# The rows of the first expert slot: gathers, stores and loads put two steps earlier, four weight pieces put later

## The chip, the cores and the metric

The kernel runs on one core of a Trainium2 chip. The metric is device time in microseconds (us), the median of several runs. The engines are named as in the profile: PE (matrix multiply), PEld (its weight loads), DVE (vector), ACT (scalar), POOL (GpSimd) and SP (the queue that issues most DMAs). Each works through its own instructions in order, and they wait for each other through semaphores.

## What is computed

Banded attention over 8 batches, 8 heads, 576 positions and 64 dimensions, then a mixture of 8 experts of which each token takes one:

```python
scores = where(mask[h], q @ k.T / 8, -1e9)      # 4 heads: window of 32; 4 heads: every 4th of 128 back
x = softmax(scores) @ v                          # -> [4608 tokens, 512]
logits = x @ w_gate + modality_bias[modality_id]
e = argmax(logits); g = max softmax(logits)
out[i] = g[i] * (relu(x[i] @ w1[e[i]]) @ w2[e[i]])   # w1: [8, 512, 1024], w2: [8, 1024, 512]
```

## The kernel before

**Attention.** The work is cut into 72 units, nine per batch; a unit is up to 128 query rows of a few heads. A step handles two units; `state['t']` is the number of the first, so it counts 0, 2, 4, ... 70, and "step 64" below is the step in which it is 64. In step t the scores of units t, t+1 are made and masked (`sm`, L438, the first DVE work of a step), those of the step before go through exp (ACT, L448), and those of two steps before are multiplied with v and normalized into `x_sb` (L399). `x_sb` has three buffers; a buffer is stored to `x_dram` in DRAM by a POOL DMA at the step's end, and the DVE may write it again only when that store has landed. The DMAs of q and k (`st`) and of v (`vw`) for the next batch are issued on SP in the same steps. After each batch its tokens are routed: the gate's logits, ranks per expert, and six POOL scatters (L632) of token numbers into `table`, one row range per expert.

**Experts.** The second phase works through slots of 256 tokens of one expert; 18 slots and a half one. Four slots are fixed early, from the first three batches. A slot's rows take this path, all in `gather`: token numbers `idt` come from `table`; four POOL DMAs gather rows of `x_dram` into `xr` (128 rows by 256 floats each); one DMA stores `xr` to `x_slot` in DRAM (512 KB); four DMAs load it back as `xg` in another layout (128 KB each). Then `prepare_x` makes the operands: for each half of the slot a DVE transpose `xt` from `xg` (L963), an ACT cast `xh` (L969) and a DVE difference `xl` (L972). For slots 0 and 1 all DMAs of `gather` are on POOL. PE multiplies `xh`, `xl` with halves of the weights (L1097, L1015); weights come by SP into `w1q` (two tiles, four pieces each for the first slot) and `w2q` (four tiles), `fetch_weights`. From step 70 on expert work is mixed with the last attention steps.

**What sets the order.** PE, DVE, ACT and SP run in the order in which the program is written; POOL too, through a chain of ordering edges. Each step calls the batch tasks three times (`advance`). One of them, `background(2)`, runs three generators side by side: `first_rows(0, ...)` and `first_rows(1, ...)`, which take the next part of `gather` when `state['t']` has reached the next number of their lists, and `first_slot`, which issues one weight piece of slot 0 at each number of its list. With `t0 = (b + 2) * 9 + 6` = 42 the list of `first_rows(0)` is 54, 55, 58, 59, 60, 62, 64: four gathers, an empty part, the store to `x_slot`, the loads of `xg`. Odd numbers come at the next even step. The twelve pieces of `first_slot` are `w2q` 0, `w1q` 0 in four parts, `w2q` 1, `w2q` 2, `w1q` 1 in four parts, `w2q` 3. DMAs of a queue take eight landing semaphores in turn, so an issue waits until the eighth DMA before it on that queue has landed.

Of the kernel before, what the change touches and what calls it, by code (L numbers as in the profile page):

```python
# [58 lines left out]
def kernel(  # L59
# [64 lines left out]
    def load_qk(b, kd, queue=nc.sync):  # L124
        kn = load_one(b, kd, k)
        return load_one(b, kd, q, queue), kn
# [24 lines left out]
    state = {('qk', 0, 0): load_qk(0, 0, nc.scalar)}  # L151
# [581 lines left out]
    def rest_info():  # L733

        eh, bh, cs = state['rest']
        yield
        state['info_h'] = yield from slot_list(eh, bh, 1, "info_h", False)
        yield
        nc.vector.memset(state['info', len(EARLY)][:, 2, NSTAT:NSTAT + 1], 1)
        state['left'] = cpool.tile([1, 1], I32, name="left")  # L740
        nc.vector.tensor_scalar(out=state['left'], in0=cs[:, 0, NE - 1:NE], scalar1=float(-NSTAT), scalar2=0.0, op0=ALU.add, op1=ALU.max)
# [51 lines left out]
    def gather(n, ids):  # L793


        idt, nu = ids
        xr = gat.tile([P, 2, DM], F32, name="xr", bufs=1)
        nrows = round_rows(n)
        queue = pool if n < 2 else nc.sync
        for u in range(nu):  # L800
            for kd in range(2):
                pool.indirect_dma_start(out=xr[:, u, 256 * kd:256 * kd + 256], out_offset=None, in_=x_dram[kd][0:nrows, :],
                                        in_offset=bass.IndirectOffsetOnAxis(ap=idt[:, u, 2 * kd:2 * kd + 1], axis=0),
                                        bounds_check=nrows - 1, oob_is_err=False)
                yield
        yield
        queue.dma_start(out=x_slot[0:P * nu, :].rearrange("(u p) c -> p u c", p=P), in_=xr[:, 0:nu])
        yield
        while 0 < n < NS and n - 1 not in taken:
            yield  # L810
        xg = gat.tile([P, 2 * KC, P], F32, name="xg", bufs=1)
        for r in range(KC):
            queue.dma_start(out=xg[BLK * r:BLK * (r + 1), 0:nu * KC],
                              in_=x_slot[0:P * nu, P * r:P * (r + 1)].rearrange("(g i) c -> i g c", i=BLK))
        state['xg', n] = xg
# [31 lines left out]
    ids_of, si_of, fetching, loads_of = {}, {}, [], {}  # L847
# [8 lines left out]
    def fetch_slot(n):  # L856

        queue = pool if n == 1 or n in round_from else nc.sync
        if n == NS - 1:
            if 'info_h' not in state:  # L860
                return False
            si_of[n] = slot_regs(state['info_h'], 0)
        else:
            r = max(r for r, n0 in enumerate(round_from) if n >= n0)
            if ('info', r) not in state:
                return False
            si_of[n] = slot_regs(state['info', r], n - round_from[r])
        ids_of[n] = fetch_ids(si_of[n], state['scatters'] if n == NEARLY else (), 1 if n == NS - 1 else 2, queue, n < NEARLY)
        return True

    def load_more(n, pieces):

        if n not in loads_of and n in si_of:
            loads_of[n] = [fetch_weights(si_of[n], n == 0), 0]
        if n in loads_of:
            for _ in range(min(pieces, 6 - loads_of[n][1])):
                next(loads_of[n][0], None)
                loads_of[n][1] += 1

    def first_rows(n, at):  # L880

        rows = gather(n, ids_of[n])
        for t in at:
            while state['t'] < t:
                yield
            next(rows, None)
            yield
        fetching.extend([(n, rows)] * n)
        todo['rows'] = max(todo['rows'], n + 1)

    def first_slot():

        prep = prepare_x(0, ids_of[0])
        for n, at in enumerate((46, 50, 52, 54, 56, 60, 62, 64, 65, 66, 67, 68)):
            while state['t'] < at:
                if state['t'] > 63:
                    next(prep, None)
                yield
            load_more(0, 1)
            loads_of[0][1] = max(n - 5, 1)  # L900
            yield
        yield from prep

    def background(b):


        if b < B - 1:
            yield
            yield
        steps = gating(b, state['lT', b])  # L910
        if b in round_of:
            for _ in steps:
                yield
                if ('counts', b) in state:
                    break
            yield from together(steps, slot_info(state['counts', b], round_of[b]))
            if round_of[b] > 0:
                return
            yield
            for n in range(2):  # L920
                fetch_slot(n)
                yield

            t0 = (b + 2) * 9 + 6
            yield from together(first_rows(0, (t0 + 12, t0 + 13, t0 + 16, t0 + 17, t0 + 18, t0 + 20, t0 + 22)), first_rows(1, (t0 + 21, t0 + 22, t0 + 24, t0 + 25)), first_slot())
            while state['t'] < NU - 4:
                yield
            state['go'] = True
            return
        yield from steps  # L930
        if b == B - 1:
            yield
            yield from slot_info(state['counts', b], len(EARLY))
            yield from rest_info()
            state['routed'] = True
# [6 lines left out]
    def together(*pieces):  # L942

        pieces = list(pieces)
        while pieces:
            for p in list(pieces):
                if next(p, pieces) is pieces:
                    pieces.remove(p)
            yield


    def prepare_x(n, ids):


        nu = ids[1]
        while ('xg', n) not in state:
            yield
        xg = state['xg', n]
        xh = xpre.tile([P, KC, SLOT], F32R, name="xh")
        xl = xpre.tile([P, KC, SLOT], F32R, name="xl")  # L960
        for u in range(nu):
            xt = xpre.tile([P, KC, P], F32, name="xt", bufs=1)
            nc.vector.transpose(out=xt.rearrange("p m (g i) -> p g m i", i=BLK),  # L963
                                in_=xg[:, KC * u:KC * (u + 1)].rearrange("p g (m c) -> p g m c", c=BLK))
            if u == nu - 1:
                taken.add(n)
            yield
            ts = slice(P * u, P * (u + 1))
            nc.scalar.copy(out=xh[:, :, ts], in_=xt)  # L969
            if n == 0:  # L970
                yield
            nc.vector.tensor_tensor(out=xl[:, :, ts], in0=xt, in1=xh[:, :, ts].bitcast(F32), op=ALU.subtract)  # L972
            if u < nu - 1:
                yield
        state['x', n] = xh, xl
# [249 lines left out]
    for t in range(NPAIR + 4):  # L1225
# [49 lines left out]
        n = NCHUNK[here[0][1]] if here and t > 1 else (0, 0)  # L1275
# [4 lines left out]
        for one in late:  # L1280
            one.gather_logits()
            if one.last:
                tasks.append((one.b, background(one.b)))
# [75 lines left out]
```

## Time and profile before

| | |
|---|---|
| median of 3 runs | 673.14 us (671.59 to 675.19) |
| the profiled execution | 676.78 us, of which its span (first to last instruction) 675.2 us |
| mean granted TensorE clock | 0.984 |
| PE, PEld busy | 635.6 us (94%), 553.1 us (82%) |
| DVE, ACT, POOL busy | 478.8, 433.5, 250.5 us |
| moved by DMAs | 99.12 MB, mean 147 GB/s |

Attention takes the first third of the span, the experts the rest. The busy shares are means over both. The profile cuts the span into 40 slices of 16.9 us; the step times and waits of the place that the change touches are read from the trace, from 140 to 262 us. Granted clock 1.00 is the higher of the two levels of TensorE's clock (2.4 GHz), 0.50 the lower (1.2 GHz).

### The profile page before, as it was taken

Reading aid. Unit: us, or ns where it says so; the run is one execution under the profiler, and the core shown is the slowest. Engines: PE = TensorE matmul, PEld = TensorE weight load, DVE = VectorE, ACT = ScalarE, POOL = GpSimd, SP = SyncE. Lnnn points to the kernel's source line nnn. Section 1 sums busy time; section 2 is a strip of 40 time slices with the busy share of each in tenths; the row PEclk is TensorE's granted clock in tenths of the full one; section 3 lists DMA queues with packets and bytes.
Section 4 is the critical chain, followed back from the end, with each engine's and each line's share of the span. In section 5 each row is a group of like instructions: output and inputs, shape, how many; then the busy total and the mean of one; then the engine's idle time right before and its main releaser. Section 6 shows DMA issues by size and latency. Waiting matters only on the chain. (4 is left out here: it accounts for less than half of the span.)

```text
span 675.2 us, 17669 instructions
## 1 busy us (share of the span) xinstructions
PE 635.6 (94%) x6398; PEld 553.1 (82%) x6398; DVE 478.8 (71%) x1068; ACT 433.5 (64%) x1002; POOL 250.5 (37%) x348
## 2 busy tenths in 40 slices
PE   7989999999994899999999999999999999999994
PEld 3778788888873787889999999999999999999973
DVE  3778868888773777956776677667766776677653
ACT  1778888888873665456566656665666566556653
POOL 8032344555664386735231321332313241321110
PEclk8999999999996999999999999999999999999998
DMA  9987776999995243965332237823222335931560
GB/s 181 211 227 184 201 155 167 204 183 234 222 274 142 72 91 123 191 163 164 110 110 80 79 111 228 209 79 110 95 95 79 109 110 147 246 108 56 136 175 13
DMA packets 121998, 99.12 MB, mean 147 GB/s; under 512 B 67424, under 2 KB 99682, under 8 KB 121908
## 3 DMA queue, kind: packets, MB, share of 16 engines
q1 hardware_dynamic: 106724, 66.56, 41.9%
q0 software_dynamic: 12144, 30.75, 15.0%
q8 instruction: 51, 0.84, 0.6%
q10 hardware_dynamic: 3040, 0.65, 0.6%
q14 instruction: 39, 0.32, 0.2%
HBM read 127.52 MB, written 29.39 MB: 232 GB/s over the span
## 5 line engine op out<-in xcount | busy, mean ns | idle before, releaser
L982 DVE TENSOR_TENSOR w2l<-w2q,w2h 128x512 fp32r<-128x512 f32 x152 | 104.4, 689 | 40.3 <-ACT w2h L981 32.3
L1015 PE MATMUL py<-w2h,hh 128*128 128x512 f32 x288 | 115.1, 400 | 0.5 <-ACT ys L1018 0.5
L313 POOL DMA_INDIRECT xr<-x_dram,idt x74 | 81.1, 1096 | 89.8 <-DMA x_slot<-xr 67.5
L1015 PE MATMUL py<-w2h,hl 128*128 128x512 f32 x288 | 113.5, 394 | 0.0
L1015 PE MATMUL py<-w2l,hh 128*128 128x512 f32 x288 | 112.3, 390 | 0.0
L313 POOL DMA_INDIRECT out_dram<-ys,idt x37 | 40.7, 1101 | 188.3 <-ACT ys L1018 123.6
L982 DVE TENSOR_TENSOR w1l<-w1q,w1h 128x512 fp32r<-128x512 f32 x152 | 103.7, 684 | 8.9 <-ACT w1h L981 8.8
L981 ACT CAST w1h<-w1q 128x512 fp32r<-128x512 f32 x152 | 94.1, 622 | 3.5 <-DMA w1q<-in_moe_w_dram 3.1
L981 ACT CAST w2h<-w2q 128x512 fp32r<-128x512 f32 x152 | 92.7, 613 | 0.0
L1097 PE MATMUL pt<-xh,w1h 128*128 128x256 f32 x304 | 86.2, 284 | 0.0
L1097 PE MATMUL pt<-xh,w1l 128*128 128x256 f32 x304 | 85.8, 282 | 0.2 <-DVE w1l L982 0.2
L1097 PE MATMUL pt<-xl,w1h 128*128 128x256 f32 x304 | 85.5, 281 | 0.0
L448 ACT ACTIVATE sm<-sm,nmx 128x96 f32<-128x96 f32 x288 | 80.5, 370 | 4.2 <-DVE nmx L444 4.2
L1103 ACT ACTIVATE hh<-pt 128x256 fp32r<-128x256 f32 x76 | 29.1, 384 | 80.7 <-PE pt L1097 80.7
L1097 PE MATMUL ph<-xh,w1l 128*128 128x256 f32 x272 | 76.7, 282 | 1.6 <-DVE w1l L982 1.6
L1097 PE MATMUL ph<-xh,w1h 128*128 128x256 f32 x272 | 76.7, 282 | 0.1
L1097 PE MATMUL ph<-xl,w1h 128*128 128x256 f32 x272 | 76.5, 281 | 0.0
L1103 ACT ACTIVATE hh<-ph 128x256 fp32r<-128x256 f32 x68 | 26.0, 383 | 71.7 <-PE ph L1097 71.7
L632 POOL DMA_INDIRECT table<-pay,dst x48 | 49.6, 1033 | 45.1 <-DVE pay L625 22.4
L1015 PEld LDWEIGHTS py<-w2l,hh 128*128 128x128 f32 x288 | 54.1, 188 | 13.4
L1015 PEld LDWEIGHTS py<-w2h,hh 128*128 128x128 f32 x288 | 54.7, 190 | 8.0 <-ACT ys L1018 0.9
L1097 PEld LDWEIGHTS pt<-xh,w1h 128*128 128x128 f32 x304 | 57.4, 189 | 3.4
(218 smaller groups left out, 1336.8 us busy)
## 6 DMA issues: line engine op xcount, KB each, us to landing
w2q<-in_moe_w_dram SPq DMA_DIRECT2D x76, 512.0 KB
w1q<-in_moe_w_dram SPq DMA_DIRECT2D x152, 256.0 KB
x_dram<-x_sb POOLq DMA_DIRECT2D x32, 256.0 KB
x_slot<-xr SPq DMA_DIRECT2D x16, 512.0 KB
xg<-x_slot SPq DMA_DIRECT2D x64, 128.0 KB
st<-in_k_dram SPq DMA_DIRECT2D x32, 144.0 KB
vw<-in_v_dram SPq DMA_DIRECT2D x16, 288.0 KB
st<-in_k_dram SPq DMA_DIRECT2D x8, 576.0 KB
```

The costliest lines, as they stand in the source:

```text
L313: ins = tc.keep_in_program_order(getattr(nc.gpsimd, name)(*args, **kw))
L448: nc.scalar.activation(out=self.sm[:, j], in_=self.sm[:, j], func=AF.Exp, bias=self.nmx[:, j])
L632: ins = nc.gpsimd.indirect_dma_start(out=table, out_offset=bass.IndirectOffsetOnAxis(ap=dst[:, c:c + 1], axis=0), in_=pay[:, b * NGB + c, ...
L981: nc.scalar.copy(out=hi, in_=raw)
L982: nc.vector.tensor_tensor(out=lo, in0=raw, in1=hi.bitcast(F32), op=ALU.subtract)
L1015: nc.tensor.matmul(out=py[u], lhsT=ht[:, us], rhs=wt, start=(f + n == 0), stop=(f + n == FC + 1))
L1097: nc.tensor.matmul(out=ph, lhsT=wt[:, c, :], rhs=xt[:, c, 0:cols], start=(c + i == 0), stop=(c + i == KC + 1))
L1103: nc.scalar.activation(out=hh, in_=ph, func=AF.Relu)
```

## The change

```diff
     def first_slot():
 
-        prep = prepare_x(0, ids_of[0])
-        for n, at in enumerate((46, 50, 52, 54, 56, 60, 62, 64, 65, 66, 67, 68)):
+        for n, at in enumerate((46, 50, 52, 54, 56, 62, 64, 64, 66, 66, 68, 68)):
             while state['t'] < at:
-                if state['t'] > 63:
-                    next(prep, None)
                 yield
             load_more(0, 1)
             loads_of[0][1] = max(n - 5, 1)
             yield
-        yield from prep
+
+    def first_x():
+
+        while state['t'] < 64:
+            yield
+        yield from prepare_x(0, ids_of[0])
...
-            yield from together(first_rows(0, (t0 + 12, t0 + 13, t0 + 16, t0 + 17, t0 + 18, t0 + 20, t0 + 22)), first_rows(1, (t0 + 21, t0 + 22, t0 + 24, t0 + 25)), first_slot())
+            yield from together(first_rows(0, (t0 + 8, t0 + 9, t0 + 10, t0 + 12, t0 + 13, t0 + 14, t0 + 18)), first_rows(1, (t0 + 21, t0 + 22, t0 + 24, t0 + 25)), first_slot(), first_x())
```

The list of `first_rows(0)` becomes 50, 51, 52, 54, 55, 56, 60: each part of `gather` for slot 0 comes two steps (four units) earlier or three (the store). `prepare_x` runs as a generator of its own, from step 64 on. The pieces `w2q` 1 and `w2q` 2 go from steps 60 and 62 to 62 and 64. Nothing is added or left out: 303 rows on POOL, 754 on SP, as before.

On POOL, from the last gather of slot 0 to its loads `xg` (steps 60 to 64), before:

```order
L313 DMA xr<-x_dram_88,idt 128x256
L632 DMA table<-pay,dst 41472x3
L313 DMA x_dram_87<-x_sb 128x2x256
L632 DMA table<-pay,dst 41472x3
L313 DMA x_slot<-xr 128x2x512
L632 DMA table<-pay,dst 41472x3
L313 TENSOR_TENSOR t_3918<-t_3918,ewt 96x48
L313 TENSOR_TENSOR ex<-l,mx 96x48
L313 DMA x_dram_87<-x_sb 64x256
L313 DMA x_dram_88<-x_sb 32x2x128 x2
L632 DMA table<-pay,dst 41472x3
L313 DMA xg<-x_slot 32x8x128 x4
```

and now, from step 56 (`sume` is a small sum of the routing) to step 60:

```order
L313 TENSOR_SCALAR sume<-sume 96x6
L313 DMA x_slot<-xr 128x2x512
L313 TENSOR_TENSOR r_3577<-oh 96x24
L313 TENSOR_TENSOR run<-run,r_3577 96x8 x3
L313 TENSOR_TENSOR t_3574<-t_3574,oh 96x48
L313 DMA x_dram_88<-x_sb 128x2x256
L632 DMA table<-pay,dst 41472x3
L313 DMA x_dram_87<-x_sb 128x2x256
L632 DMA table<-pay,dst 41472x3
L313 DMA xg<-x_slot 32x8x128 x4
L632 DMA table<-pay,dst 41472x3
L313 DMA x_dram_87<-x_sb 128x2x256
```

The four gathers stand ahead of this piece; the last of them stands where the first stood, and `xg` stands where the last gather stood, ahead of the store of `x_sb` that ends the piece.

On DVE, from the `nmx` of step 64 to the first `xl`, before:

```order
L444 TENSOR_REDUCE nmx<-sm 128x8
L469 TENSOR_SCALAR den<-po 128x8
L470 RECIPROCAL den<-den 128x8
L399 TENSOR_TENSOR x_sb<-po,den 128x2x2x64 x2
L514 COPY lT<-po 64x4x32
L514 COPY lT<-po 64x4x16
L518 TENSOR_TENSOR lT<-po,lT 64x2x32
L149 COPY vw_109<-vw_109 32x520 x2
L963 STREAM_TRANSPOSE xt<-xg 128x4x4x32
L584 TENSOR_REDUCE m_4053<-t_3918 96x6
L586 TENSOR_TENSOR oh<-ewt,m_4053 96x48
L972 TENSOR_TENSOR xl<-xt,xh 128x4x128
```

and now, from the `sm` of step 64:

```order
L438 TENSOR_TENSOR sm<-pss,masks 128x768
L965 STREAM_TRANSPOSE xt<-xg 128x4x4x32
L444 TENSOR_REDUCE nmx<-sm 128x8
L469 TENSOR_SCALAR den<-po 128x8
L470 RECIPROCAL den<-den 128x8
L399 TENSOR_TENSOR x_sb<-po,den 128x2x2x64 x2
L514 COPY lT<-po 64x4x32
L514 COPY lT<-po 64x4x16
L518 TENSOR_TENSOR lT<-po,lT 64x2x32
L149 COPY vw_109<-vw_109 32x520 x2
L974 TENSOR_TENSOR xl<-xt,xh 128x4x128
L584 TENSOR_REDUCE m_4054<-t_3922 96x6
```

The transpose has moved from the end of step 64 to just behind the step's `sm`; the second one moves likewise, to just ahead of the `sm` of step 66.

On SP, the loads of steps 58 to 62, before:

```order
L121 DMA st<-in_k_dram 96x4x384
L121 DMA st<-in_q_dram 96x4x384
L833 ISA
L833 DMA w2q_246<-in_moe_w_dram 128x2x512
L141 DMA vw_107<-in_v_dram 64x4x128 x2
L141 DMA vw_107<-in_v_dram 16x4x128
L141 DMA vw_107<-in_v_dram 48x4x128
L141 DMA vw_107<-in_v_dram 64x4x128
L141 DMA vw_107<-in_v_dram 32x4x128
L833 ISA
L833 DMA w2q_247<-in_moe_w_dram 128x2x512
```

and now:

```order
L121 DMA st<-in_k_dram 96x4x384
L121 DMA st<-in_q_dram 96x4x384
L141 DMA vw_107<-in_v_dram 64x4x128 x2
L141 DMA vw_107<-in_v_dram 16x4x128
L141 DMA vw_107<-in_v_dram 48x4x128
L141 DMA vw_107<-in_v_dram 64x4x128
L141 DMA vw_107<-in_v_dram 32x4x128
L833 ISA
L833 DMA w2q_246<-in_moe_w_dram 128x2x512
L833 ISA
L833 DMA w2q_247<-in_moe_w_dram 128x2x512
```

One weight tile of 512 KB has gone behind the last v loads of attention; the rest of SP's order is the same. PE's order is the same from end to end.

## Rows read from the trace of the kernel before

**Rows 1.** The page, the span in 40 slices: PE's busy tenths and granted clock.

```profile
PE   7989999999994899999999999999999999999994
PEclk8999999999996999999999999999999999999998
```

**Rows 2.** Waits, 150 to 262 us: who waited for whom, total, times, longest.

```profile
DVE xt L963 <- DMA xg<-x_slot: 9.7, 1, 9.7
...
DVE x_sb L399 <- DMA x_dram<-x_sb: 3.1, 2, 1.9
...
POOL table L632 <- DMA table<-pay,dst: 1.2, 1, 1.2
```

**Rows 3.** Timeline of DVE: start, us, instruction, [idle before it <-what ended that].

```profile
195.02 0.42 DVE L399 TENSOR_TENSOR x_sb<-po,den 128x256 f32<-128x256 f32 x1 [1.23 <-DMA x_dram<-x_sb]
...
197.98 0.96 DVE L438 TENSOR_TENSOR sm<-pss,masks 128x768 f32<-128x768 f32 x1 [0.75 <-ACT ux L482]
...
200.27 0.75 DVE L399 TENSOR_TENSOR x_sb<-po,den 128x256 f32<-128x256 f32 x2
...
212.11 0.71 DVE L963 STREAM_TRANSPOSE xt<-xg 128x512 f32<-128x512 f32 x1 [9.72 <-DMA xg<-x_slot]
```

**Rows 4.** Timeline of POOL, same columns; a DMA's us are its issue.

```profile
172.00 1.12 POOL L313 DMA_INDIRECT xr<-x_dram,idt  x1 [0.30 <-issue]
...
177.90 0.24 POOL L313 TENSOR_SCALAR sume<-sume 96x6 f32<-96x6 f32 x1
...
185.64 0.78 POOL L313 DMA_DIRECT2D x_dram<-x_sb  x1
186.72 0.96 POOL L632 DMA_INDIRECT table<-pay,dst  x1 [0.30 <-issue]
187.99 1.05 POOL L313 DMA_INDIRECT xr<-x_dram,idt  x1 [0.30 <-issue]
...
190.28 0.78 POOL L313 DMA_DIRECT2D x_dram<-x_sb  x1
...
196.16 0.74 POOL L313 DMA_DIRECT2D x_slot<-xr  x1 [3.84 <-DMA xr<-x_dram,idt]
...
204.05 2.35 POOL L313 DMA_DIRECT2D xg<-x_slot  x4 [2.41 <-DMA x_slot<-xr]
```

**Rows 5.** Steps 46, 48, 50; 62, 64, 66, 68: length, busy times, PEclk, DMA share, GB/s.

```profile
145.60:150.84 5.24, 5.24 (x104) 4.44 (x102) 4.89 (x19) 5.24 (x16) 3.44 (x7) 1.00 0.87 222
150.84:155.74 4.90, 4.90 (x105) 4.35 (x103) 4.43 (x12) 4.47 (x13) 1.97 (x8) 1.00 0.96 210
155.74:160.45 4.71, 4.71 (x102) 4.16 (x100) 4.51 (x14) 4.62 (x14) 0.73 (x1) 1.00 1.18 256
...
189.55:197.98 8.43, 6.98 (x115) 5.66 (x116) 4.77 (x13) 4.75 (x14) 3.97 (x5) 1.00 1.11 259
197.98:214.11 16.13, 6.89 (x144) 5.80 (x140) 5.88 (x15) 6.41 (x19) 9.65 (x15) 0.78 0.90 243
214.11:220.12 6.01, 5.98 (x63) 4.92 (x65) 4.96 (x15) 4.52 (x13) 2.25 (x8) 0.50 0.00 0
220.12:225.40 5.28, 5.28 (x111) 4.50 (x110) 5.08 (x15) 4.28 (x13) 1.14 (x2) 0.96 0.24 78
```

**Rows 6.** DMA queues, 185 to 190 us: packets, MB, share; q1 SP's, q0 POOL's.

```profile
q1 hardware_dynamic: 795, 1.15, 103.4%
q0 software_dynamic: 4, 0.01, 1.0%
```

**Rows 7.** Timelines of SP, PE and ACT: a q load, its user; a weight load, its user.

```profile
184.00 0.43 SPq L121 DMA_DIRECT2D st<-in_q_dram  x1
184.62 0.45 SPq L833 DMA_DIRECT2D w2q<-in_moe_w_dram  x1
...
194.83 0.55 PE L351 MATMUL pss<-ident,st 96*128 96x96 f32 x4 [1.45 <-DMA st<-in_q_dram]
...
236.93 0.62 ACT L981 CAST w2h<-w2q 128x512 fp32r<-128x512 f32 x1
```

**Rows 8.** Busy time by stretch (columns of rows 5), late in the expert phase.

```profile
600.00:650.00 50.00, 50.00 (x317) 45.08 (x317) 34.78 (x61) 29.41 (x61) 4.21 (x4) 1.00 0.42 117
```

## The prediction

> **What bounds the kernel now.** I read the page's slices first. PE is busy nine tenths or more in nearly every slice, but slice 13 (203 to 219 us) has a 4, and the granted clock dips only there [rows 1]. So there is one hole, at the seam between attention and the experts. Late in the expert phase PE is busy 50.00 of 50 us [rows 8]: nothing there absorbs time, and expert work follows in the same order on every engine, so what the seam gains or loses reaches the end in full. Second, the waits around the hole: the longest is the DVE's first transpose `xt`, 9.7 us for the loads of `xg` [rows 2]. Third, the DVE's timeline: the transpose starts at 212.11, behind 9.72 us of idleness, so the DVE had nothing to do from 202.4 [rows 3]. DVE runs in order, so the next scores' mask, and with it exp and PE, stand behind it. The step took 16.13 us; its counterpart two batches earlier, step 46, took 5.24 [rows 5]. Fourth, POOL, to see why `xg` is late. The last gather was issued at 187.99, the store to `x_slot` had to wait for it until 196.16, the loads had to wait for that until 204.05, the transpose could start at 212.11 [rows 4, 3]. So each of the three links takes 8.17, 7.89 and 8.06 us from issue to use: a chain of 24.1 us that starts too late. The DMA share in those steps is 0.90 to 1.11 [rows 5]: the 16 engines are full, which is why the links are so long and why bringing something forward can cost something else.
>
> **The change part by part.**
>
> *The gathers and the store.* The last gather now stands on POOL where the first stood, at 172.00. The store stands behind `sume`, which ends at 177.90 + 0.24 = 178.1 [rows 4]. With the measured links: gathered by 172.0 + 8.2 = 180.2, so the store goes out at 180.2, not at 178.1, and POOL waits 2 us for it. It lands by 180.2 + 7.9 = 188.1. A delay can come ahead of that: POOL's DMAs take eight landing semaphores in turn, and two more gathers now stand close ahead of the four stores at the end of step 52. Such a wait cost 1.2 us in the trace [rows 2]; it is paid zero to two times, so the last gather goes out between 172 and 174.5.
>
> *The loads of `xg`.* They stand behind the scatter that ends at 186.72 + 0.96 = 187.7. With the store landed by 188.1 they go out then, and land by 188.1 + 8.1 = 196.2; with the 2.5 us of delay, 198.7. The transpose now stands behind the `sm` of step 64, which ends at 197.98 + 0.96 = 198.9 [rows 3]. Both are in time. The term: **9.7 us less** wait.
>
> *The clock.* PE stood still during the wait, and in step 66 its granted clock was 0.50, in step 68 0.96 [rows 5]. Those steps took 6.01 and 5.28 us, their counterparts 4.90 and 4.71: together 1.7 us more [rows 5]. Part of that is work that stands there for another reason: the second transpose, a cast and a difference. Without the long stop the clock stays up. The gain lies between 0 and 1.7; I take 0.9, the middle, since `prepare_x` adds to each of the two steps an operation as long as the 0.71 us transpose [rows 3].
>
> *What is late next, first the store of `x_sb`.* The store issued at 190.28 [rows 4] now stands behind the four `xg` issues (2.35 us) and no longer behind a gather (1.05): 191.6. The buffer that it frees is written by the DVE at 200.27 [rows 3]. How long such a store takes under this load is seen one store earlier: issued at 185.64 [rows 4], waited for until 195.02 [rows 3], 9.4 us. That gives 201.0, 0.7 us late. Moreover 512 KB of `xg` stand ahead of it in POOL's queue; at the 259 GB/s of step 62 [rows 5] these are 2.0 us. The cost lies between 0 and 2.7; I take 1.2.
>
> *Next, the q load of the last batch.* PE waited for it until 194.83, already 1.45 us [rows 7], and it now shares the DMA engines with the store to `x_slot` and with `xg`, 1.05 MB that used to move after it. At most they take 1.05 MB / 259 GB/s = 4.0 us ahead of it. At least nothing: from 185 to 190 us, when this load was under way, POOL's queue moved 4 packets and SP's 795 [rows 6]. Two of the four gathers, 256 KB, have also left this stretch. I take 1.8, near the 2.0 us of the store alone, since `xg` goes out when this load is already moving.
>
> The Trainium skill (Trainium Kernel Development and Optimization, section Key Constraints) speaks against a free gain here: DMAs issued from SP, ACT and POOL run on the same 16 engines and interleave. The full share in rows 5 agrees; by that sentence alone the whole 4.0 us would be charged and the sum would be 2.2 us smaller.
>
> *The weight pieces.* `w2q` 1 used to be issued at 184.62, right behind the q load, and is first read by the cast at 236.93 [rows 7], so 52 us early. It goes behind the v loads, at most some 10 us later, and the cast comes about 8 us earlier: still over 30 us of cover. It gives the v loads 2.0 us of engine time, which nobody waits for: 0. Without that cover it would cost what it is late. The four other pieces keep their order on SP: 0.
>
> *`prepare_x` in the middle of a step.* Two transposes, two casts, two differences, as before. They stand ahead of `nmx` and so on the way to exp: at most one transpose, 0.71 us [rows 3], is added to step 64's own way, but before, three such operations stood behind the wait on the same way. 0.
>
> *Slot 1.* Its gathers keep their steps; they used to go out inside the hole and now go out between attention's stores. Its `xg` is read a whole slot later than slot 0's, so this is covered: 0.
>
> Sum: -9.7 - 0.9 + 1.2 + 1.8 = **-7.6 us**. Against the profiled execution, 676.78 us (span 675.2): 669.2. That execution lies 3.6 us above the median of the runs; the median goes from 673.14 to 673.14 - 7.6 = **665.5**. The ends: -9.7 - 1.7 = -11.4, so 661.7; -9.7 + 2.7 + 4.0 = -3.0, so 670.1.
>
> **The rivals.**
>
> *A. POOL's queue is held up.* The store of `x_slot` goes out at 180.2, and rows 6 show that between 185 and 190 POOL's queue moves almost nothing. What was issued at 185.64 was there at 195.02 [rows 4, 3]. If part of the store misses the gap before 185, it lands with that one, at 195.0. Then `xg` goes out at 195.0 and lands at 203.1; the transpose waits 203.1 - 198.9 = 4.2 us in place of 9.7, and the store of `x_sb`, now at 198.5, frees its buffer up to 3 us after the DVE asks for it. Gain 9.7 - 4.2 - 1.5 + 0.5 = 4.5 us, with half of those 3 us and half a microsecond of the clock: 668.6. For it: rows 6. Against it: 5 us from 180.2 to 185 are enough for 512 KB at half the engines' rate, 4.0 us. The Trainium skill (DMA: Bandwidth & Descriptors, section Queues, rings and completion order) has each engine take the queues that have work in turns, a packet from each. By that rule the store would not be held up and A would fall away; rows 6 do not agree with it, so A keeps its chance.
>
> *B. It does not do what it says.* The rows arrive no earlier when it matters: the gathers go out earlier but queue behind the loads, and what the transpose no longer waits for is waited for at the q load and the store of `x_sb`. With those two at their ends (4.0 + 2.7) and the transpose still waiting 2 us, the gain is about 1 us: 672. For it: the DMA share is full on both sides. Against it: the data that expert weights bring (2.5 MB, issued from 184 us on) is not read before 236.93 [rows 7] and can give way.
>
> *C. Slower: the store of `x_sb` behind `xg`.* POOL runs in order. While `xg` waits for `x_slot`, the next `x_sb` store waits too, and with three buffers the DVE must have it at 200.27. If the store of `x_slot` landed no earlier than now, `xg` would go out at 204.05 to 206.4 [rows 4], the `x_sb` store at 207.6, and it would be there at 217: step 64 would stand still for 16.7 us in place of 9.7. 7 us more: 680. It decides from the point where that store lands 9.7 us late, at 210: `xg` out at 197.1, so `x_slot` 17 us under way where 7.89 was measured [rows 4]. Nothing in the trace takes that long.
>
> **How the numbers follow.** The forecast 0.60, A 0.24, B 0.11, C 0.05. A measurement of this kernel can tell about 0.5% (3.4 us) from no change. Faster by more than that means below 669.8: nearly all of the forecast (0.58), most of A (0.19), some of B (0.02): 0.79. Within it: the rest of these, 0.17. Slower: C less its mild half, 0.04. The range runs from the best end of the forecast (661.7, taken as 661.5) over its worst and over A to 671.0; it leaves out C, most of B and little else.
>
> **What would show each step.** The DVE's wait for `xg` gone or under 1 us, and step 64 near 7 to 8 us in place of 16.13: the main term. Granted clock 1.00 throughout the slices from 203 to 237 us: the clock term. A new wait of the DVE's `x_sb` for `x_dram` in step 64, of 0 to 3 us: the store's term; PE's wait for `st<-in_q_dram` grown from 1.45 to about 3: the load's. POOL's `xg` going out near 188 is the forecast, near 195 is A, behind 200 is C. The prediction is wrong if the `xg` wait stays above 5 us, if the two new waits pass 6 us together, or if the expert phase, from the first PE work on `xh` to the end, is more than 1 us longer than before.

## The result, and the profile after

The changed kernel took 668.62 us (median of 17 runs, 664.7 to 681.23) where the kernel before took 677.46 in the same session (median of 17, 671.59 to 684.69). The ratio is 0.9887, 95% interval 0.986 to 0.9914. On the median that the forecast started from this is 673.14 x 0.9887 = 665.5 us, 7.6 us less: the forecast.

The executions that were profiled with this result and with `prep_only` below ran slower than the rest (spans 679.6 and 694.1 us, mean clocks 0.976 and 0.959), and the ratios leave such runs out. So the rows of the change come from two later profiled executions of the same kernel, runs `change_again` and `change_third`; the second was on another chip, and the kernel before was profiled there too, as `before_third`. Spans and mean granted clocks, in this order:

```profile
core 0: 673.5 us, clock 0.986
```

```profile
core 0: 676.4 us, clock 0.987
```

```profile
core 0: 686.0 us, clock 0.978
```

**The hole.** First the DVE's timeline of `change_again` in step 64, which answers to [rows 3]:

```profile
201.84 0.96 DVE L438 TENSOR_TENSOR sm<-pss,masks 128x768 f32<-128x768 f32 x1 [5.82 <-PE pss L436]
202.72 0.70 DVE L965 STREAM_TRANSPOSE xt<-xg 128x512 f32<-128x512 f32 x1
203.34 0.91 DVE L444 TENSOR_REDUCE nmx<-sm 128x8 f32<-128x768 f32 x1
...
204.60 0.75 DVE L399 TENSOR_TENSOR x_sb<-po,den 128x256 f32<-128x256 f32 x2
```

The transpose has no bracket: nothing was waited for, where 9.72 us stood before. `x_sb`, two rows below, has none either. But the step's first row has a new one, 5.82 us for PE's scores. Next POOL in the same run, which answers to [rows 4]:

```profile
170.78 1.09 POOL L313 DMA_INDIRECT xr<-x_dram,idt  x1 [0.30 <-DMA xr<-x_dram,idt]
...
176.28 0.81 POOL L313 DMA_DIRECT2D x_slot<-xr  x1
...
185.92 2.35 POOL L313 DMA_DIRECT2D xg<-x_slot  x4
```

`xg` went out at 185.92, 18 us sooner than at 204.05, and without waiting for `x_slot`. (Step 62 of this execution began at 189.20, 0.35 us sooner than in [rows 5], so 185.92 corresponds to 186.3 there; in `change_third` it was 196.48, with step 62 8.9 us later than in [rows 5], which corresponds to 187.6.) Last the steps 62, 64, 66 and 68 of `change_again`, and of `change_third`, which answer to [rows 5] and have its columns:

```profile
189.20:201.84 12.64, 8.58 (x120) 7.14 (x120) 4.78 (x13) 5.36 (x16) 7.62 (x12) 0.86 1.10 269
201.84:208.37 6.53, 5.84 (x114) 4.83 (x111) 6.32 (x16) 6.42 (x20) 2.82 (x3) 1.00 1.03 245
208.37:213.73 5.36, 4.28 (x85) 3.47 (x84) 4.92 (x15) 4.26 (x13) 1.05 (x5) 1.00 0.36 123
213.73:218.56 4.83, 4.61 (x102) 4.04 (x102) 4.57 (x14) 3.28 (x9) 2.13 (x3) 1.00 0.26 85
```

```profile
198.42:205.75 7.33, 6.93 (x116) 5.64 (x116) 4.70 (x14) 4.33 (x12) 5.03 (x9) 1.00 0.85 177
205.75:212.81 7.06, 6.24 (x114) 5.00 (x112) 6.40 (x17) 6.06 (x19) 5.83 (x8) 1.00 1.04 274
212.81:218.82 6.01, 4.70 (x91) 3.75 (x91) 4.95 (x13) 5.36 (x16) 1.57 (x6) 1.00 0.85 229
218.82:223.67 4.85, 4.62 (x102) 4.05 (x102) 4.59 (x15) 3.29 (x9) 2.13 (x3) 1.00 0.27 88
```

Step 64 is 6.53 and 7.06 us where it was 16.13. I call these four steps together the seam; it took 35.9 us before [rows 5], and 29.4 and 25.2 us now. Step 62, 8.43 before, is 12.64 in one execution and 7.33 in the other. Why is seen on PE in `change_again`, which answers to [rows 7]:

```profile
197.17 0.90 PE L351 MATMUL pss<-ident,st 96*128 96x96 f32 x4 [4.06 <-DMA st<-in_q_dram]
```

The wait for the last q load has grown from 1.45 to 4.06 us.

**The expert phase** was longer in these two executions, though its program is the same: 449.8 us from the end of step 68 to the end of the span before, 454.9 and 452.7 now. (Two further executions of the kernel before, in the table below, took 450.5 and 451.9, so about 2 us of such a difference need no change.) The first operations of the first slot show where. Stretches of 5 us around the first `w2h` products (columns of [rows 5]), from the kernel before, from `change_again`, and from `before_again`, the kernel before on the chip of `change_third`:

```profile
235.90:240.90 5.00, 5.00 (x62) 4.28 (x61) 2.83 (x5) 4.13 (x13) 4.82 (x8) 1.00 0.38 105
```

```profile
229.06:234.06 5.00, 4.74 (x36) 4.16 (x38) 3.24 (x7) 3.76 (x11) 4.63 (x8) 0.67 0.37 105
```

```profile
248.56:253.56 5.00, 5.00 (x48) 4.29 (x47) 2.96 (x5) 3.76 (x11) 4.82 (x8) 0.66 0.38 108
```

Each stretch begins 10.5 us behind the end of step 68. PE is nearly always busy in it, yet at a granted clock of 0.67 and 0.66, between its two levels of 1.2 and 2.4 GHz, it ran 36 and 48 operations where at 1.00 it ran 62. Just ahead of this PE had stood 2.4 us for `hl`, in the executions with the fall and in those without. From the end of step 68 to the third transpose of `xt`, which stands in the first slot, took 18.6 us before (225.40 to 243.98) and 20.5 in both executions of the change, 1.9 us more. Some 1.5 us of this is the lower level: `before_again`, the kernel before with the fall, took 20.1 (238.06 to 258.14). Of the runs below the fall is also in `weights_only`, `store_twice`, `xg_later` and `w1_later`, but not in `all_later` and `w1_later_again`, and in `rows_only` the clock fell in step 68 instead (0.57). So it can't be put down to the change alone.

In `change_third` the second slot adds 0.9 us, and the slots from the third on together take what they took before, to 0.3 us. In `change_again` the third and fourth slot together add another 2.2 us: ACT waited for results on their way to `out_dram`, and the clock fell once more behind this, to 0.72 from 290 to 295 us.

```profile
ACT ys L1020 <- DMA out_dram<-ys,idt: 2.6, 1, 2.6
```

### The profile page after: what moved, and what is told of

It reads as the page before. It is cut to its first block, busy times and chain, and to the rows that moved or that the text cites. A ratio compares the mean times of both kernels' runs of the same rounds, so it can differ in the third digit from the quotient of the medians.

```text
span 679.6 us, 17668 instructions
## 1 busy us (share of the span) xinstructions
PE 641.3 (94%) x6397; PEld 557.8 (82%) x6398; DVE 480.1 (71%) x1068; ACT 433.5 (64%) x1002; POOL 250.3 (37%) x348
## 5 line engine op out<-in xcount | busy, mean ns | idle before, releaser
L1017 PEld LDWEIGHTS py<-w2l,hh 128*128 128x128 f32 x288 | 54.1, 188 | 13.3
```

What stands on the lines that cost most here:

```text
L1017: nc.tensor.matmul(out=py[u], lhsT=ht[:, us], rhs=wt, start=(f + n == 0), stop=(f + n == FC + 1))
```

## The experiments

Two theories were set against each other first. Theory S, that of the forecast: the rows that come sooner take the `xg` wait away, and this alone is the gain. Theory W: the gain comes from the weight pieces, which leave the DMA engines to others. The change has three parts, rows, weight list and the transpose's place (`first_x`, ahead of `nmx`), and these kernels have some of them; the transpose's new place is in all of them, so no run has the sooner rows with the old place. All diffs are against the changed kernel. The table gives for each run the ratio to the kernel before on the same chip, and of its one profiled execution step 56 with its granted clock, steps 62 and 64, the seam, the expert phase, and the DVE's wait for `xg`, in us.

| run | ratio (95%) | 56 (clock) | 62 | 64 | seam | expert phase | `xg` wait |
|---|---|---|---|---|---|---|---|
| before | 1 | 6.0 (1.00) | 8.4 | 16.1 | 35.9 | 449.8 | 9.7 |
| before_again | 1 | 9.6 (0.65) | 6.2 | 15.7 | 32.9 | 450.5 | 9.2 |
| before_third | 1 | 9.5 (0.64) | 6.2 | 14.6 | 32.0 | 451.9 | 8.1 |
| change_again | 0.9865 (0.980 to 0.993) | 7.0 (1.00) | 12.7 | 6.5 | 29.4 | 454.9 | 0 |
| change_third | 0.9793 (0.974 to 0.985) | 6.1 (1.00) | 7.3 | 7.1 | 25.2 | 452.7 | 0 |
| rows_only | 0.9885 (0.983 to 0.994) | 9.1 (0.65) | 8.6 | 8.9 | 29.4 | 451.2 | 0 |
| weights_only | 1.0033 (0.999 to 1.007) | 6.2 (1.00) | 12.8 | 17.4 | 40.2 | 450.8 | 10.5 |
| prep_only | 1.0067 (1.003 to 1.010) | 9.3 (0.64) | 7.0 | 20.7 | 38.2 | 453.3 | 13.8 |
| store_twice | 0.9872 (0.979 to 0.995) | 9.3 (0.64) | 6.8 | 6.8 | 26.1 | 452.3 | 0 |
| xg_later | 0.9972 (0.991 to 1.003) | 6.1 (1.00) | 13.8 | 6.5 | 30.5 | 456.1 | 0 |
| all_later | 0.9868 (0.980 to 0.994) | 6.1 (1.00) | 7.6 | 9.2 | 27.1 | 451.7 | 2.6 |
| w1_later | 0.9826 (0.974 to 0.992) | 6.2 (1.00) | 8.1 | 6.6 | 26.0 | 452.6 | 0 |
| w1_later_again | 0.9820 (0.975 to 0.989) | 9.6 (0.65) | 6.8 | 7.2 | 24.0 | 450.0 | 0 |

**The changed kernel again**, unedited, beside the next three.

> The changed kernel once more, for a profile that is not disturbed. Theory S (the rows' chain starts 16 us earlier, so the transpose no longer waits 9.7 us for xg; part of it comes back at the q load and the store of x_sb, which share the DMA engines): 7 to 8 us less than before, ratio 0.989; no wait for xg over 1 us, the two new waits 3 to 6 us together. Theory W (the gain comes from the 512 KB weight tile that left its place ahead of the last v loads): the same time, but v loads that land 2 us or more earlier and PE or DVE waits for them that are gone.

674.89 us, against 680.66 for the kernel before, run beside it. Its rows are those above. The wait for `xg` is gone, as theory S has it; the two new waits came to 2.6 us together (none for `x_sb`), a little under the 3 to 6 expected.

**The rows with the transpose's new place**, and the old list of weights:

```diff
-        for n, at in enumerate((46, 50, 52, 54, 56, 62, 64, 64, 66, 66, 68, 68)):
+        for n, at in enumerate((46, 50, 52, 54, 56, 60, 62, 64, 65, 66, 67, 68)):
```

> The rows earlier and prepare_x as a task of its own, but the weight pieces in their old steps. Theory S: most of the gain stays, 5 to 8 us less than before (0.988 to 0.993), since the weight tile stands behind the q load that PE waits for. Theory W: 0 to 3 us less.

673.55 us, as much gained as with the whole change. Steps 62 and 64:

```profile
191.25:199.82 8.57, 6.99 (x119) 5.77 (x119) 4.71 (x14) 6.55 (x21) 4.13 (x6) 1.00 1.10 238
199.82:208.73 8.91, 7.72 (x159) 6.65 (x155) 6.61 (x18) 6.73 (x20) 7.65 (x11) 1.00 1.06 271
```

The hole is closed without the new list. From `prep_only` below this run differs in the rows alone, and there the time is 682.5 us. So theory S stands, and the list, which the forecast put at nothing, is worth nothing that this shows.

**The weights with the transpose's new place**, and the old rows:

```diff
-first_rows(0, (t0 + 8, t0 + 9, t0 + 10, t0 + 12, t0 + 13, t0 + 14, t0 + 18))
+first_rows(0, (t0 + 12, t0 + 13, t0 + 16, t0 + 17, t0 + 18, t0 + 20, t0 + 22))
```

> The weight pieces later and prepare_x as a task of its own, but the rows in their old steps. Theory S: 0 to 2 us less (xg shares with less, 2 us of engine time at most), the transpose still waits 7 to 10 us for xg. Theory W: 4 us or more less.

682.81 us, no gain. The waits show that the hole is as it was:

```profile
DVE xt L965 <- DMA xg<-x_slot: 10.5, 1, 10.5
```

Theory W falls. Beside `prep_only` (next), which has the old list as well, the new list makes no difference either: 682.81 and 682.5 us.

**The transpose's place alone**: both edits above, so that old rows and old weights are left.

> Only prepare_x as a task of its own (the transpose just behind the scores' mask of step 64); rows and weight pieces in their old steps. Theory S: no change, within 2 us; the wait for xg only moves to an earlier place in the DVE's order and grows by what no longer runs ahead of it, some 3 us. A theory that the order on DVE and ACT brings the gain: 3 us or more less.

682.5 us, 0.67% slower than before, the whole interval above 1: 4.6 us, where theory S had 2 at most. The wait and step 64 in the profiled execution:

```profile
DVE xt L965 <- DMA xg<-x_slot: 13.8, 1, 13.8
```

```profile
209.64:230.35 20.71, 7.05 (x108) 5.37 (x106) 6.49 (x16) 8.35 (x26) 9.82 (x15) 0.69 0.70 193
```

The transpose now stands ahead of `nmx`, so what it waits for is waited for by exp as well. `weights_only`, with the same place and the old rows, shows it too: 10.5 us of waiting and a step 64 of 17.4 us. The new place is free only when the rows are there; it is a stake that the sooner rows have to cover.

**The store twice.** This run and the next three were on a second chip. Was the longer step 62 the store and `xg` ahead of the q load, as the forecast's last term has it (theory E)? A second store of the same 512 KB, which nothing reads, doubles the suspect:

```diff
+        if n == 0:
+            queue.dma_start(out=x_twice[0:P * nu, :].rearrange("(u p) c -> p u c", p=P), in_=xr[:, 0:nu])
```

> The changed kernel, and the 512 KB store to x_slot issued a second time into a tensor that nobody reads (work added, nothing left out): it doubles what POOL's queue moves ahead of the last q load. Theory E (the load and the rows share full engines, so the load lags by what is moved ahead of it): PE's wait for the q load grows by 2 us (512 KB at 259 GB/s), step 62 from 12.7 to 14.7 us, and the time is 1 to 3 us over the changed kernel. Theory Q (POOL's queue is hardly served while the q load moves, so the lag has another cause): step 62 unchanged within 0.7 us, but x_slot and xg land later and the transpose waits again.

672.33 us, ratio 0.9872, no dearer as far as one can see. The two stores on POOL, and step 62:

```profile
178.07 0.82 POOL L314 DMA_DIRECT2D x_slot<-xr  x1 [1.16 <-DMA xr<-x_dram,idt]
178.89 0.75 POOL L314 DMA_DIRECT2D x_twice<-xr  x1
...
190.81 2.55 POOL L314 DMA_DIRECT2D xg<-x_slot  x4
```

```profile
194.36:201.15 6.79, 6.79 (x116) 5.66 (x116) 4.69 (x13) 2.99 (x7) 3.24 (x6) 1.00 0.91 185
```

PE is busy for all of step 62, and the transpose does not wait, so neither theory's signs are there. But this doesn't decide on theory E. The execution had lost time in steps 54 and 56 (10.1 and 9.3 us, 5.5 and 7.0 in `change_again`), so PE came to the load some 15 us after its issue (183.03 to about 198.1); in `change_again` it was there after 14.0 (183.19 to 197.17). So it was at most 1.1 us later than there, where E expected 2; among loads that took 10.8 to 14.0 us in other executions (see below) that is too near to settle. Nor does the ratio's interval, 0.979 to 0.995, exclude the 1 to 3 us of E.

**`xg` one step (two units) later**, so that it goes out behind the q load rather than with it:

```diff
-first_rows(0, (t0 + 8, t0 + 9, t0 + 10, t0 + 12, t0 + 13, t0 + 14, t0 + 18))
+first_rows(0, (t0 + 8, t0 + 9, t0 + 10, t0 + 12, t0 + 13, t0 + 14, t0 + 20))
```

> The changed kernel with the loads of xg one step later (step 62 in place of 60), behind the store of x_sb; gathers and the store to x_slot stay early. Theory E: PE's wait for the q load shrinks by 1 to 2 us, and xg, issued some 6 us later, lands about 4 us after it is asked for: the transpose waits 2 to 5 us and the time is 0 to 3 us over the changed kernel. A theory that the store of x_sb behind xg is what costs: the DVE's waits for x_dram go and the time falls by 1 to 2 us.

681.71 us, ratio 0.9972: the expectation, at most 3 us over the changed kernel, missed. Step 62, and from the waits the expert phase's new one:

```profile
185.46:199.24 13.78, 9.69 (x114) 8.00 (x114) 4.79 (x14) 6.57 (x20) 9.68 (x15) 0.77 1.07 249
```

```profile
ACT ys L1020 <- DMA out_dram<-ys,idt: 4.8, 1, 4.8
```

Nothing waited for `xg`, but step 62 was long all the same (PE waited 2.9 us for the q load and 1.2 for the k load), and the third slot stood still for 4.8 us behind its own results. Against the first profile of the kernel before, the seam gave 5.4 us in this one execution and the expert phase took 6.3 back. This execution, at 673.68 us, was the fastest of the ten, so it doesn't show what cost the others their gain; that is open.

**Weights later.** If not the rows, then perhaps the weight pieces lie ahead of the q load. One kernel, `all_later`, puts off all five pieces that were issued ahead of step 60, the other, `w1_later`, two of them:

```diff
-        for n, at in enumerate((46, 50, 52, 54, 56, 62, 64, 64, 66, 66, 68, 68)):
+        for n, at in enumerate((60, 60, 60, 62, 62, 62, 64, 64, 66, 66, 68, 68)):
```

> The changed kernel with w2q 0 and all parts of w1q 0 (1.5 MB) put to steps 60 and 62, behind the q load. Theory E: 1.5 MB / 259 GB/s = 5.8 us of engine time leave the stretch before the load: steps 52 to 62, 42.8 us in the changed kernel, shrink by 4 to 6 us and PE's wait for the q load is gone; 3 to 6 us less than the changed kernel (0.978 to 0.984 of before). Rival L (weights late): the first expert casts wait for w1q 0, issued from about 184 us on and due at some 212; then 0 to 3 us less, or none.

```diff
-        for n, at in enumerate((46, 50, 52, 54, 56, 62, 64, 64, 66, 66, 68, 68)):
+        for n, at in enumerate((46, 50, 52, 60, 60, 62, 64, 64, 66, 66, 68, 68)):
```

> The changed kernel with two of the four parts of w1q 0 (512 KB) put from steps 54 and 56 to step 60, behind the q load. Theory E: PE's wait for the q load shrinks by about 2 us, step 62 from 12.7 to about 10.7, 1 to 3 us less than the changed kernel (0.984 to 0.986 of before). Theory Q: no change.

672.12 us (0.9868) and 670.63 us (0.9826). Step 62 of either:

```profile
188.65:196.23 7.58, 7.10 (x116) 5.72 (x117) 4.69 (x14) 4.32 (x12) 5.44 (x8) 1.00 1.11 227
```

```profile
190.06:198.12 8.06, 7.37 (x119) 5.85 (x119) 4.71 (x14) 5.23 (x16) 3.34 (x5) 1.00 1.14 251
```

Both are short, but the ratio of the first is not the 0.978 to 0.984 that theory E expected, though its interval (0.980 to 0.994) reaches there. With all pieces late, 2.6 us of the `xg` wait came back, and POOL waited 2.6 us for the store to `x_slot`; that the weights' bytes collide with the rows there is likely, but was not tested.

**Is `w1_later` better than the change?** On a third chip both were run side by side, and the kernel before was profiled twice more. Theory N says that there is no difference.

> The kernel before once more, for a second profile: in the first one the expert phase, from the scores' mask of step 70 to the last instruction, takes 449.8 us, in the profiles of the changed kernel 452.2 and 454.9. Theory V (executions differ: in some the clock falls for 3.4 us in the first slots, with a loss of 1.5 us each): this phase takes 449.8 to 454 us here too, and steps 62 and 64 together stay at 22 to 28 us with a wait for xg of 8 to 12 us. Theory G (part of the gain is given back in the first slots): 449.5 to 451 us again.

> The same kernel, a third profile. Theory V: the expert phase between 449.8 and 454 us, and not the same as in the second by 1 us or more. Theory G: 449.5 to 451 us.

> The changed kernel, a third profile. No wait for xg over 1 us; steps 62 to 68 together 28 to 33 us against 35.9. Theory V: expert phase 450 to 455 us. Theory G: 452 us or more. Time 0.984 to 0.991 of before.

> The changed kernel with two parts of w1q 0 behind the q load, again, beside the changed kernel on one chip. Theory E (the q load lags by what is moved ahead of it): 1 to 4 us less than the changed kernel in this call, step 62 under 10 us. Theory N (the first result was chance): the same as the changed kernel within 1 us.

676.59 us for the change and 676.84 for `w1_later`, with the kernel before at 690.11: the same, as theory N has it. No version was found that beats the changed kernel. The expert phases of the kernel before, 450.5 and 451.9 us, speak for theory V: theory G had both at 451 at most. `change_third` has 452.7 there; its seam, 25.2 us, and its ratio, 0.9793, are better than expected (28 to 33 us, 0.984 to 0.991).

The gain on this chip is larger, 13.5 us. Part of the difference is seen in steps 54 and 56, first of `before_third`, then of `change_third`.

```profile
172.11:180.89 8.78, 6.64 (x124) 5.54 (x120) 4.52 (x13) 6.15 (x19) 7.40 (x11) 1.00 0.81 201
180.89:190.43 9.54, 8.66 (x96) 6.91 (x97) 4.58 (x13) 4.07 (x10) 4.54 (x10) 0.64 0.97 189
```

```profile
175.70:182.21 6.51, 5.90 (x108) 5.14 (x108) 4.53 (x12) 6.04 (x19) 5.46 (x7) 1.00 1.17 245
182.21:188.35 6.14, 6.05 (x120) 4.92 (x117) 4.59 (x13) 5.14 (x15) 4.06 (x9) 1.00 0.94 210
```

18.3 us against 12.7: of the 9.6 us between the two spans, 6.8 come from the seam and 5.7 from these steps, and the rest goes the other way. The first profile of the kernel before had these steps in 13.2 us. They are not the change's doing in any way that was tested: `w1_later_again`, with the sooner rows, took 16.8 us in them, `rows_only` 16.8 and `store_twice` 19.3, on three chips.

What differs is the clock. Step 56 takes 9.1 to 9.6 us in six of the thirteen executions of the table, each time at a granted clock of 0.64 or 0.65, and 6.0 to 7.0 us at 1.00 in the other seven; both kinds are found on each of the three chips. Step 56 of `rows_only` and of `weights_only`, with the same number of PE operations:

```profile
172.33:181.42 9.09, 9.09 (x125) 7.71 (x123) 4.58 (x13) 5.90 (x18) 5.12 (x9) 0.65 0.95 184
```

```profile
172.42:178.57 6.15, 6.15 (x125) 5.07 (x123) 4.58 (x15) 5.49 (x16) 4.89 (x10) 1.00 0.99 193
```

The lower clock costs 2.9 us here. What lets it fall is open: PE had stood 2.0 us in step 54 of `rows_only`, and 1.9 us in step 54 of `xg_later`, where the clock stayed at 1.00.

**When PE waits in step 62.** In none of the six executions with a long step 56 did PE wait for the q load in step 62: it comes later to the load when it has lost time ahead of it. In the four that waited (`before`, `change_again`, `weights_only`, `xg_later`) PE asked for the load 9.4 to 10.5 us after its issue on SP, and it was there 10.8 to 14.0 us after. In the other nine PE came about 11.6 to 18.4 us after the issue. What sets the 10.8 to 14.0 us was not tested. The sooner rows alone are not it, for `weights_only`, with the old rows, has 13.3 (183.44 to 196.73).

## Why the prediction was right, step by step

*The bound.* Right. The one hole was the wait for `xg`, and taking it away shortened the run; a wait of 9.7 us gave 7.6.

*The main term, -9.7.* Right. Step 64 fell by 9.6 us in `change_again` and by 7.5 from `before_third` to `change_third`. The chain was worked out with links of about 8 us and `xg` at 188; set to step 62 of the earlier rows it went out at 186.3 and 187.6. (Two of the gathers, like the store, moved three steps, not two.)

*The clock, -0.9.* Right where it was looked for, incomplete beyond. Steps 66 and 68 took 10.2 and 10.9 us instead of 11.3. But the sign that I gave, 1.00 in all of 203 to 237, did not come true: the lower level turned up in the first slot instead, some 1.5 us. It did so with the kernel before as well, in one execution of three. So the term should have been near zero with a width of 2 us to either side. This, and the wait for `out_dram`, are also much of why one of my three signs of error came true: from the first PE work on `xh` to the end it took 448.6 us in the first profile of the kernel before, 453.1 in `change_again` and 451.0 in `change_third`, more than 1 us longer. The sign was too narrow, since `before_third` took 450.8.

*The store of `x_sb`, +1.2.* Mis-sized: 0. In step 64 neither execution has a wait ahead of `x_sb`. In `change_again` that says little, since the DVE came 4 us later for another reason, the q load. In `change_third` it does; the store on POOL behind `xg`, and the DVE's write:

```profile
200.31 0.75 POOL L313 DMA_DIRECT2D x_dram<-x_sb  x1
```

```profile
208.50 0.75 DVE L399 TENSOR_TENSOR x_sb<-po,den 128x256 f32<-128x256 f32 x2
```

The store was there within 8.2 us, where I had 9.4, taken from the store before it, and up to 2.0 more for `xg` ahead of it. What was true of one store was no guide to the next.

*The q load, +1.8.* Mis-sized and differently caused. In `change_again` the wait grew by 2.6 us and step 62 by 4.2, above my upper end of 4.0; in `change_third` step 62 was 1.2 us longer than in `before_third` on the same chip (7.33 against 6.18), with no wait for the load. The step that was missing is how late PE comes to the load: the term took it to come as in the first profile, 9.4 us after the issue, and it came 13.7 us after it in `change_third` and some 15 in `store_twice`, without a wait. For the load's own time `change_again` has 14.0 us, 3.2 more than before; but `weights_only` has 13.3 without the sooner rows. So that the store and `xg` cause it, as the term says, isn't shown. The Trainium skill (Trainium Kernel Development and Optimization, section Key Constraints) has the DMAs of all queues share the 16 engines; DMA shares of 1.10 and 1.03 in steps 62 and 64 of `change_again` agree, but that alone does not say which transfer gives way.

*The weights and `prepare_x`, 0 each.* The weights: right as far as the runs can tell, by `rows_only` against `change_again` and `weights_only` against `prep_only`. (Of the four numbers of the list that changed, two are odd ones that come at the next even step anyway; what moved is `w2q` 1 and `w2q` 2, and in SP's order `w2q` 1 alone.) `prepare_x`: right only together with the rows; alone its new place costs 0.7%, by `prep_only`. The forecast should have named this as what it costs when the cover is gone.

*The sum.* Terms of either sign were off and roughly cancelled: no cost at `x_sb` (1.2 us better than forecast), step 62 longer by 1.2 to 4.2 us (forecast 1.8), the expert phase by 0.8 to 5.1 (forecast 0; `change_third` against `before_third`, `change_again` against the first profile). The seam, of which the sum speaks, is 6.5 and 6.8 us shorter in these two pairs, near the 7.6; the spans differ by 1.7 and 9.6 us, the rest lying outside it. That the sum hit 665.5 to the tenth is partly luck; the range of 9.5 us was what the terms supported.

*The rivals.* A did not come true: POOL did not wait for `x_slot`, and `xg` went out near 188, not at 195. But its premise held. From 186 to 190 us of `change_again`, with `xg` issued from 185.92 on, POOL's queue moved as little as in [rows 6]:

```profile
q1 hardware_dynamic: 559, 0.85, 105.6%
q0 software_dynamic: 34, 0.01, 1.7%
```

In `rows_only`, where `xg` went out at 189.54, it is 2 packets against 486 from 189.5 to 193 us. The store to `x_slot` (176.28) escaped this: it had landed by 185.92, since POOL's `xg` did not wait for it. The Trainium skill (DMA: Bandwidth & Descriptors, section Queues, rings and completion order) has an engine take queues that have work in turns; these rows don't show such turns, though the trace does not tell when POOL's DMAs were ready to move. B falls in general, with 7.6 us gained, but its mechanism, that the gain comes back at the q load, is what one sees in `xg_later` and partly in `change_again`. C falls: nothing waited behind `xg`.

*What stays open.* What sets how long the q load takes; how far the lower clock in the first slot has to do with the change; what lets the clock fall in step 56 in some executions; why the gain on the third chip is larger, since `w1_later_again`, with a long step 56, gained as much (0.9820); and what the sooner rows would give with the transpose in its old place.

## What to carry to other kernels

When one engine that runs in order stands before a load, follow the chain of issues back and move its first link, not its last: here three links of 8 us each had to start sooner. An operation moved ahead into a chain's way is free only as long as its data are there, so test the move without the earlier data too. Terms for "who gives way on full DMA engines" deserve wide bounds in both directions, since they differ from execution to execution by more than their mean.

## What was not expected of the hardware

- A second store of 512 KB into DMA engines with a share near 1 (1.05 and 1.01 in steps 54 and 56) cost nothing that four runs could measure (0.9872, 0.979 to 0.995).
- In `change_again` POOL's queue stood nearly still for 4 us while SP's moved 0.85 MB, though loads of `xg` had been issued on POOL (34 packets against 559).
- PE ran 36 to 48 operations in 5 us at a granted clock of 0.66 to 0.67 where it ran 62 at 1.00, in the same place of the program, behind the same stop of 2.4 us, in some executions and not in others.
- The executions of one kernel spread with their mean granted clock: of the first session's, those of the changed kernel took 664.92 us at 0.994, 667.79 at 0.986, 671.51 at 0.987 and 674.25 at 0.982. What lowers the clock in one and not in the other is not settled.
- Step 56 takes 6.0 to 7.0 us at a granted clock of 1.00 and 9.1 to 9.6 us at 0.64 or 0.65, each on all three chips. In none of the six executions with the lower clock did PE wait for the q load in step 62.
